# A new order of steps, W rows spread by TensorE, and no warm-up transposes in a three-network kernel

## The chip, the cores and the metric

The kernel runs on one core of one Trainium2 chip. The metric is the time of one execution on the device in microseconds (us). Five engines work side by side, each through its own queue in order: TensorE (PE: matmuls, with weight loads as PEld), VectorE (DVE), ScalarE (ACT), GpSimd (POOL) and SyncE (SP), which here issues all DMA transfers.

## The reference

Three parts follow one another. First a recurrent attention over 4 batches x 8 heads x 768 positions with head size 40:

```
m_new = max(f[t] + m, i[t])
C = exp(f[t] + m - m_new) * C + exp(i[t] - m_new) * outer(v[t], k[t])
n = exp(f[t] + m - m_new) * n + exp(i[t] - m_new) * k[t]
y[t] = sigmoid(o_gate[t]) * (C q[t]) / max(|n q[t]|, 1)
```

Its output, 3072 tokens x 320 features, goes into the first network: `h = x @ w_in` (320 to 1024), `s = h * softmax(h)`, a layer norm of s with gain `g_ln`, and `@ w_out` (1024 to 320). Then the second network: `g = x @ w_gate`, `val = x @ w_val` (320 to 1536 each), and `(silu(g) * val) @ w_out` (1536 to 320). Weights of the two networks come as 64-bit floats.

## The kernel before, in words

**Tiles.** The 768 positions are cut into 6 chunks of 128. A tile j is one chunk of one batch: j = 4 * chunk + batch, 24 tiles in all. Tiles 0 to 3 belong to the first chunk. In the second network four tiles (512 tokens) form a group g, and 128 of the 1536 hidden features form a slice f; a unit (g, f) is one of 6 x 12 = 72.

**The order is written by hand.** Every step is a small function, and the string ORDER (lines 28 to 101) lists which step is issued when, as `name:tile`, up to unit 18. A third number picks the engine for steps that can run on two: 0 is VectorE, 1 is GpSimd. After the string, `program` (line 104) goes on by rule: for each further unit gv, gt, gw, gy, yh, yl and then o2 of the unit before. Nothing reorders the steps later: each engine runs its share of this list in this sequence, and waits where an operand or a buffer isn't ready.

**The steps**, with the engine that runs them and the line in the profile:

- Gates of a chunk c: g0, g1, g2, gs (scans and small sums; L276 to L304), gd (store of the row gl to DRAM), gc and gx (transpose on PE, L318, then copy and exp into columns), er and ed (factors for the state).
- Decay weights W of a tile: gb loads the 8 rows gl of the tile from DRAM, spread over 128 partitions (512 KB, L340); gm masks them on GpSimd (L343); we takes 8 exponentials on ScalarE (L350).
- Attention of a tile: ld_qk, ld_vo, ld_qx, ld_e (loads); sc (scores on PE, L365), pm (times W on VectorE, L369), pv, pi, pd (matmuls, L377, L383, L391), cs, cd, ca (state), r0 to r2, ya, yb, yd (normalization, L420 to L439).
- First network of a tile: xT (transposes, L444), xh and xl (split in two parts of less precision), h (16 matmuls, L467), hx (maximum, DVE L471), he (exp, ACT), hu (DVE L480), z0, z1, zm, hc (DVE), hv (ACT), hr (GpSimd), uT (8 transposes, L513), uh and ul (split), o (24 matmuls, L530), oe, xd, x2, xc (output and transposes).
- Weights of the first network: w1l and w2l load them, five and four chunks; w1a to w1d and w2a to w2d turn the 64-bit pattern into float32 (ACT L183; DVE L187, L191, L196); w1h, w1o, w2h, w2o split them.
- Second network: vl, va to vd, vh, vo load, convert and split the weights of slice f (12 slices; vo is L678 and L680), Xh and Xl split the input, gv (16 matmuls, L707), gt, gw, gy (L711, L715, L719), yh, yl (L723, L727), o2 (12 matmuls, L737), ev (output). p2a and p2b mark where memory of the earlier parts becomes free for weights of the second network.
- wu: 8 transposes of the identity into a PSUM tile that nobody reads (L636). There are 18 of them.

**Buffers.** PSUM has two tiles of two banks, from `bank2` (they hold sc, h, uT and gv), and four of one bank, from `bank1`. A step that needs a slot waits for the last reader of the tile that held it. W has three slots in SBUF, qk and kvo four each.

The steps of the W path are these, and the change touches them:

```
def gb(j):
    c, b = divmod(j, B)
    T["W", j] = ak.tile([128, H, L], F32, tag="W", name="W", bufs=3)
    sp.dma_start(out=T["W", j], in_=gdr[c][b * H:(b + 1) * H, :].partition_broadcast(128))
```

Of the kernel before, what the change touches and what calls it, by code (L numbers as in the profile page):

```python
# [28 lines left out]
im w1l:0 ld_rows wu:0 ld_qk:0 w2l:0 wu:1 w1a:0 w1l:1 g0:0 w1b:0 g1:0:0 wu:2 g2:0 g0:1 gd:0 gs:0 w1c:0 ld_qk:1 wu:3  # L29
w2a:0 w1d:0 w2l:1 wu:4 w1h:0 w2b:0 w2c:0 w1o:0 gb:0 gc:0 sc:0 w1l:2 gx:0 w2d:0 w1a:1 g1:1 w1b:1 w2h:0 w1c:1 wu:5  # L30
ld_qk:2 w2a:1 g2:1 wu:6 w1d:1 w2b:1 w1h:1 wu:7 g0:2 gm:0 gb:1 w2c:1 w2l:2 wu:8 ld_vo:0 gs:1 we:0 w1o:1:0 gd:1 sc:1
w2d:1 w2o:0 wu:9 pm:0 w1a:2 gm:1 gb:2 wu:10 w2h:1 ld_qk:3 w1b:2 w1l:3 wu:11 g0:3 we:1 w1c:2 gc:1 w2o:1 w1d:2 pv:0
w2a:2 pm:1 er:1 gx:1 th:0 gm:2 gb:3 w1h:2 w2b:2 wu:12 ld_vo:1 w2c:2 g1:2 we:2 sc:2 r0:0 r1:0 r2:0 w2d:2 w1l:4 vw:0
ya:0 wu:13 yb:0 w1a:3 sc:3 pm:2 gm:3 gb:4 w2h:2 ld_qk:4 ib w1b:3 we:3 ld_vo:2 yd:0:0 w1c:3 pd:0 w2l:3 w2o:2 wu:14
w1o:2 w1d:3 xT:0 w1a:4 pv:1 vw:1 xh:0 w1b:4 w1h:3 cs:0 gm:4 th:1 w1c:4 ge:1 ld_qk:5 pd:1 r0:1 w1d:4 gb:5 w1o:3 sc:4
xl:0 w1h:4 ld_vo:3 g2:2 pm:3 vw:2 th:2 pv:2 gs:2 r1:1 w1o:4:0 w2a:3 we:4 r2:1 ld_qk:6 w2b:3 h:0 r0:2 ya:1 r1:2 cs:1
gm:5 yb:1 gb:6 gn:1 pm:4 yd:1 we:5 vw:3 ld_vo:4 r2:2 ed:1 ya:2 g1:3 xT:1 ld_qx:4 hx:0 gc:2 sc:5 gx:2 w2c:3 xh:1 pd:2
yb:2 ld_qk:7 w2d:3 pv:3 xl:1 gm:6 he:0 pd:3 ld_e:4 r0:3 we:6 r1:3 pv:4 hu:0 ld_vo:5 gb:7 pm:5 ld_qx:5 zm:0 sc:6 th:3
r2:3 z0:0 w2h:3 h:1 z1:0 pm:6 qw:4 ld_e:5 th:4 hc:0 gd:2 ld_qk:8 cs:2 hv:0 ya:3 yb:3 w2o:3 uT:0 ld_qx:6 pv:5 hx:1 uh:0
gb:8 vw:4 ld_vo:6 yd:2 ul:0 he:1 ld_e:6 gm:7 pi:4 th:5 qw:5:0 o:0 we:7 r0:4 g0:4 g2:3 hu:1 ld_qx:7 hr:0 zm:1:0 z0:1  # L40
ld_qk:9 cs:3 r1:4 gm:8 r2:4 sc:7 z1:1 ya:4 hc:1 pi:5 ld_vo:7 yb:4 gb:9 pd:4 we:8 r0:5 ld_qx:8 r1:5 uT:1 pm:7 ld_e:7
pv:6 r2:5 cd:4 er:2 qw:6 uh:1 ed:2 ya:5 ld_qk:10 sc:8 cs:4 vw:5 oe:0 yd:3:0 gd:3 hv:1 yb:5 pi:6 cd:5 ul:1 xT:2 vw:6
pd:5 gs:3:0 pv:7 xh:2 gm:9 gb:10 th:6 r0:6 ld_vo:8 xl:2 r1:6 ld_e:8 pm:8 h:2 we:9 r2:6 g1:4 ya:6 ld_qk:11 yb:6 th:7
ld_qx:9 qw:7:0 sc:9 ca:4 hx:2 xT:3 gm:10 o:1 pm:9 he:2 xd:0 ld_e:9 we:10 gb:11 cs:5 z0:2 hu:2 pi:7 hr:1 pv:8 ld_qk:12
z1:2 r0:7 ca:5 zm:2:0 r1:7 r2:7 ld_qx:10 hc:2 xh:3 vw:7 ld_vo:9 ya:7 th:8 sc:10 qw:8 er:3 xl:3 yb:7 uT:2 gm:11 g2:4
ld_e:10 pm:10 hv:2 gc:3 pi:8 gb:12 qw:9 pd:6 uh:2 h:3 hr:2 ul:2 gx:3 g0:5 r0:8 r1:8 r2:8 oe:1 ya:8 vw:8 ld_qk:13 we:11
cs:6 o:2 yb:8 cd:6 ld_e:11 hx:3 yd:4 gb:13 gm:12 ld_vo:10 gs:4:0 he:3 pd:7 x2:0 hu:3 pv:9 xc:0 g1:5 oe:2 ld_qk:14 z0:3
ca:6:0 we:12 ed:3 z1:3 cs:7 ld_qx:11 sc:11 zm:3 gd:4 cd:7 hc:3 pi:9 qw:10 xT:4 r0:9 sc:12 r1:9 xh:4 r2:9 ld_vo:11 vw:9
pm:11 pv:10 th:9 gb:14 ya:9 pd:8 pm:12 th:10 uT:3 yb:9 pi:10 ca:7 uh:3 xl:4 ge:2 h:4 r0:10 xd:1 th:11 qw:11 hv:3
yd:5:0 r1:10 vw:10 ld_qk:15 r2:10 gn:2 ya:10 cd:8 ld_e:12 ul:3 hr:3 ld_qx:12 gb:15 yb:10 o:3 gm:13 xd:2:0 hx:4 gm:14  # L50
cs:8 he:4 we:13 z0:4 hu:4 xT:5 sc:13 ld_qx:13 z1:4 g2:5 x2:1 ld_vo:12 zm:4 pv:11 hc:4 ld_e:13 oe:3 xh:5 we:14 xl:5
pd:9 pm:13 cd:9 ge:3 uT:4 gm:15 gb:16 pi:11 h:5 xd:3 ld_qx:14 r0:11 r1:11 cd:10 xc:1 r2:11 ld_vo:13 ya:11 uh:4
ld_qk:16 cd:11 yb:11 yd:6 ul:4 hv:4 ca:8:0 o:4 hx:5 th:12 we:15 hr:4 cs:9 ca:9 gm:16 qw:12:0 gn:3 x2:2 he:5 pd:10
# [757 lines left out]
```

## Time and profile before

| | |
|---|---|
| time, median of 3 runs | 765.88 us (765.79 to 766.67) |
| the profiled execution's own time | 765.78 us |
| its span, first to last instruction | 764.1 us |
| mean granted TensorE clock | 0.982 |
| TensorE busy | 738.7 us, 97% |
| VectorE busy | 444.2 us, 58% |
| ScalarE busy | 327.1 us, 43% |
| GpSimd busy | 176.1 us, 23% |

The profile is of one execution. Busy time is the union of an engine's instructions; matmuls overlap one another at their ends, so the spacing of their starts is their cost in a dense stretch, and it is less than the duration of one. The granted clock is given as a share of 2.4 GHz; its two levels are 1.00 and 0.50.

### The profile page before, as it was taken

How to read it: one execution, taken by the hardware profiler on the slowest of the kernel's cores; microseconds unless marked ns; L12 is line 12 of the kernel's file. 1: busy time of each engine (PE TensorE's matmuls, PEld its weight loads, DVE VectorE, ACT ScalarE, POOL GpSimd, SP SyncE). 2: the span in 40 equal slices, each digit the busy share in tenths (PEclk: the TensorE clock that was granted, in tenths of full speed). 3: DMA queues.
4: the chain of work that ended last, by engine and by line, in shares of the span. 5: the costliest groups of instructions: out<-in, count | busy, mean ns of one | idle time of the engine just before them, and what ended most of it. 6: DMA issues, size and time to landing. Idle time of an engine off the chain costs nothing. (4 is left out here: it accounts for less than half of the span.)

```text
span 764.1 us, 11503 instructions
## 1 busy us (share of the span) xinstructions
PE 738.7 (97%) x4478; PEld 658.1 (86%) x4478; DVE 444.2 (58%) x753; ACT 327.1 (43%) x675; POOL 176.1 (23%) x237
## 2 busy tenths in 40 slices
...
GB/s 235 313 231 176 236 229 146 136 277 95 139 110 68 77 104 104 103 54 51 9 148 1 0 35 1 1 35 0 1 35 1 0 1 36 1 0 36 1 1 34
DMA packets 24279, 62.31 MB, mean 82 GB/s; under 512 B 3195, under 2 KB 11488, under 8 KB 24224
## 3 DMA queue, kind: packets, MB, share of 16 engines
...
q8 instruction: 35, 0.57, 0.3%
...
## 5 line engine op out<-in xcount | busy, mean ns | idle before, releaser
L707 PE MATMUL a<-Xh,w 128*128 128x512 f32 x720 | 237.8, 395 | 3.5 <-DVE t L719 2.6
L707 PE MATMUL a<-Xl,w 128*128 128x512 f32 x432 | 169.8, 393 | 0.0
L707 PEld LDWEIGHTS a<-Xh,w 128*128 128x128 f32 x720 | 132.2, 188 | 29.5 <-ACT w L674 2.3
L715 DVE SCALAR_TENSOR_TENSOR t<-t,a 128x512 f32<-128x512 f32 x72 | 49.5, 687 | 167.4 <-ACT t L711 167.4
L737 PE MATMUL c<-w,yh 128*128 128x320 f32 x576 | 127.9, 309 | 1.1 <-ACT yh L723 1.1
L711 ACT ACTIVATE t<-a 128x512 f32<-128x512 f32 x72 | 43.0, 598 | 166.1 <-PE a L707 164.9
L737 PEld LDWEIGHTS c<-w,yh 128*128 128x128 f32 x576 | 99.1, 188 | 7.3 <-ACT yh L723 1.4
L707 PEld LDWEIGHTS a<-Xl,w 128*128 128x128 f32 x432 | 81.3, 188 | 19.3
L737 PE MATMUL c<-w,yl 128*128 128x320 f32 x288 | 89.0, 309 | 0.2 <-DVE yl L727 0.2
L723 ACT ACTIVATE yh<-t 128x512 fp32r<-128x512 f32 x72 | 45.5, 632 | 100.7 <-DVE t L719 100.7
L727 DVE TENSOR_TENSOR yl<-t,yh 128x512 fp32r<-128x512 f32 x60 | 43.2, 720 | 38.5 <-ACT yh L723 38.5
L530 PE MATMUL c<-wo_h,uh 128*128 128x320 f32 x192 | 60.5, 315 | 0.1
L350 ACT ACTIVATE W<-W,col 128x128 f32<-128x128 f32 x192 | 58.4, 393 | 4.9 <-POOL W L343 4.9
L530 PE MATMUL c<-wo_h,ul 128*128 128x320 f32 x192 | 59.6, 311 | 0.7 <-DVE ul L521 0.7
L467 PE MATMUL a<-wi_h,xh 128*128 128x512 f32 x144 | 59.6, 414 | 0.2 <-DVE P L369 0.2
L530 PE MATMUL c<-wo_l,uh 128*128 128x320 f32 x192 | 59.3, 309 | 0.0
L467 PE MATMUL a<-wi_h,xl 128*128 128x512 f32 x144 | 57.8, 401 | 0.0
L737 PEld LDWEIGHTS c<-w,yl 128*128 128x128 f32 x288 | 54.1, 188 | 0.4 <-DVE yl L727 0.4
L719 DVE SCALAR_TENSOR_TENSOR t<-t,a 128x512 f32<-128x512 f32 x72 | 49.4, 687 | 2.4
L377 PE MATMUL c<-kvo,P 128*128 128x41 f32 x384 | 49.1, 291 | 1.7 <-issue 1.7
L377 PEld LDWEIGHTS c<-kvo,P 128*128 128x128 f32 x384 | 48.1, 204 | 2.3 <-issue 1.8
L369 DVE TENSOR_TENSOR P<-a,W 128x1024 f32<-128x1024 f32 x24 | 29.1, 1214 | 24.3 <-PE a L365 16.3
...
## 6 DMA issues: line engine op xcount, KB each, us to landing
...
```

The lines of the kernel that those rows point to most:

```text
L350: act.activation(g[:, h, :], g[:, h, :], AF.Exp, bias=cols[c][:, b * H + h:b * H + h + 1])
L369: dve.tensor_tensor(out=T["P", j], in0=T["S", j].rearrange("p (h n) -> p h n", h=H), in1=T["W", j], op=ALU.mult)
L377: pe.matmul(po[:, h * D1:(h + 1) * D1], P[:, h, :], vn[:, h, :], start=h == 0, stop=j < B and h == H - 1)
L467: pe.matmul(ph[:, fs], x, w[:, fs], start=n == 0, stop=n == 7)
L530: pe.matmul(po[:, 0:DM], x[:, fs], w[:, f, :], start=n == 0, stop=n == 3 * KF - 1)
L707: pe.matmul(p[:, s * 512:s * 512 + GT], w, x, start=n == 0, stop=n == 7)
L711: act.activation(T["t", g, f], T["gv", g, f][:, 0:GT], AF.Tanh, scale=0.5)
L715: dve.scalar_tensor_tensor(out=t, in0=t, scalar=1.0, in1=p[:, 0:GT], op0=ALU.add, op1=ALU.mult)
L719: dve.scalar_tensor_tensor(out=t, in0=t, scalar=0.5, in1=p[:, 512:512 + GT], op0=ALU.mult, op1=ALU.mult)
L723: act.activation(T["yh", g, f], T["t", g, f], AF.Copy)
L727: alu[e].tensor_tensor(out=T["yl", g, f], in0=T["t", g, f], in1=T["yh", g, f].bitcast(F32), op=ALU.subtract)
L737: pe.matmul(T["acc", g][t][:, 0:DM], x[:, ts], w, start=f == 0 and n == 0, stop=f == KF2 - 1 and n == 2)
```

## The change

The ORDER string is replaced up to unit 18. The set of steps is the same but for the 18 wu, which go, together with their function. Many small steps change their engine number: in sum VectorE takes from GpSimd four g1, one gs, one w1o, three vo, four yl, six zm and two yd, and gives it five ca, four xd and two qw. `gd:0`, the store of the first chunk's gl, stays, although no load reads it any more.

For the tiles 0 to 3, W is made differently. gb no longer loads: it runs 8 matmuls into a two-bank PSUM tile, each with one column of the identity, repeated 128 times, as the stationary operand and gl of the chunk as the moving one, so that each row of gl appears on all 128 partitions. we reads that PSUM tile and writes W in SBUF, and gm masks after the exponential, with 0 as fill instead of -1e30. In the code:

```diff
     def gb(j):
         c, b = divmod(j, B)
+        if j < NP:
+
+            T["gw", j] = bank2()
+            for h in range(H):
+                n = b * H + h
+                pe.matmul(T["gw", j][:, h * L:(h + 1) * L], ident[0:BH, n:n + 1].to_broadcast([BH, 128]), T["gl", c],
+                          start=True, stop=True)
+            return
         T["W", j] = ak.tile([128, H, L], F32, tag="W", name="W", bufs=3)
         sp.dma_start(out=T["W", j], in_=gdr[c][b * H:(b + 1) * H, :].partition_broadcast(128))
 
     def gm(j):
+
         pool.affine_select(out=T["W", j], in_=T["W", j], pattern=[[0, H], [1, L]], compare_op=ALU.is_ge,
-                           fill=NEG, base=0, channel_multiplier=-1)
+                           fill=0.0 if j < NP else NEG, base=0, channel_multiplier=-1)
 
     def we(j):
         c, b = divmod(j, B)
+        if j < NP:
+            T["W", j] = ak.tile([128, H, L], F32, tag="W", name="W", bufs=3)
         g = T["W", j]
+        x = T["gw", j].rearrange("p (h n) -> p h n", h=H) if j < NP else g
         for h in range(H):
-            act.activation(g[:, h, :], g[:, h, :], AF.Exp, bias=cols[c][:, b * H + h:b * H + h + 1])
+            act.activation(g[:, h, :], x[:, h, :], AF.Exp, bias=cols[c][:, b * H + h:b * H + h + 1])
...
-    def wu(n):
-        p = bank1()
-        for i in range(8):
-            pe.transpose(p[:, (i % 4) * 128:(i % 4 + 1) * 128], ident, ident)
```

(`NP` is 4, `BH` is 32 rows.) The new order begins like this, up to the first h:

```
w1l:1 w1l:0 g0:0 g1:0:0 w2l:0 ld_rows w1a:1 w1a:0 g2:0 w1b:1 w1c:1 w1d:1 gb:1 w1b:0 w2a:0 ib gs:0 ld_qk:1 w1c:0 w1h:1
w1l:2 gc:0 w2l:2 ld_vo:0 w2b:0 gx:0 g0:1 w2c:0 g0:2 g1:1:0 w2d:0 g2:1 gs:1:0 gb:0 we:1 we:0 w1o:1 w2h:0 gm:1 sc:1 gm:0
pm:1 w1d:0 gc:1 w2a:2 gb:2 ld_qk:0 ld_vo:1 we:2 w2b:2 w2c:2 w2o:0 w1a:2 w1h:0 w2d:2 gb:3 vw:0 gx:1 w2h:2 pd:0 w2l:1
w1b:2 gd:1 sc:0 w1o:0:0 pm:0 ld_vo:2 ld_qk:2 pv:1 ld_qk:3 w1l:4 pv:0 im w2a:1 w2o:2 cs:0 w1c:2 w2b:1 w1d:2 w2c:1 r0:0
we:3 vw:1 w1l:3 gm:2 r1:0 pd:1 er:1 ld_vo:3 w2d:1 sc:2 vw:2 r0:1 gb:4 th:0 r2:0 ld_qk:4 sc:3 r1:1 ya:0 gm:3 ed:1 r2:1
ld_vo:4 pm:2 g1:2 w2h:1 ge:1 cs:1 yb:0 w1a:4 w2o:1 pm:3 yd:0:0 vw:3 w1b:4 pd:2 gn:1 pv:2 w1c:4 cs:2 w1a:3 th:2 xT:0
r0:2 th:1 ya:1 gd:0 w1d:4 gb:5 yb:1 ld_qx:4 pv:3 xh:0 w1b:3 pd:3 r1:2 w1h:2 xl:0 w1h:4 gm:4 r2:2 ya:2 yd:1 ld_e:4
w1c:3 we:4 w1d:3 w1o:2:0 xT:1 w1h:3 yb:2 w1o:4 ld_qk:5 th:3 g2:2 ld_vo:5 sc:4 w1o:3:0 g0:3 gb:6 h:0 pm:4 gs:2 xh:1
```

From there on the first network's tiles and the attention of later tiles are interleaved as before. From `x2:2 he:5 pd:10` on (line 53 before) the two orders run the same steps, up to `h:11 zm:10:0 z1:10` (line 69 before), except for wu and for the engine of some ca; then they differ again.

## Rows read from the trace of the kernel before

**Rows 1.** The page's busy line: us (share of the span) and instructions of each engine.

```profile
PE 738.7 (97%) x4478; PEld 658.1 (86%) x4478; DVE 444.2 (58%) x753; ACT 327.1 (43%) x675; POOL 176.1 (23%) x237
```

**Rows 2.** Chain of waits, in order of time: start us, us, what.

```profile
461.57 3.74 PE a L707 x16
```

**Rows 3.** Windows: stretch, busy us (instructions) of each engine, clock, DMA share, GB/s.

```profile
0.00:100.00 100.00, 86.25 (x635) 79.28 (x636) 75.81 (x154) 56.86 (x150) 57.46 (x75) 0.86 0.75 237
0.00:10.00 10.00, 7.41 (x40) 7.18 (x40) 4.31 (x15) 1.96 (x2) 3.27 (x11) 1.00 0.66 202
20.00:30.00 10.00, 2.35 (x14) 2.12 (x12) 7.34 (x14) 4.97 (x15) 9.68 (x6) 0.72 1.02 345
30.00:40.00 10.00, 10.00 (x59) 8.89 (x60) 8.28 (x13) 9.81 (x31) 9.43 (x15) 0.50 0.84 289
60.00:70.00 10.00, 10.00 (x44) 8.61 (x44) 5.44 (x11) 1.15 (x2) 4.94 (x8) 0.57 0.71 200
372.00:420.00 48.00, 45.23 (x228) 38.71 (x229) 43.91 (x52) 26.98 (x48) 19.96 (x15) 1.00 0.17 62
```

**Rows 4.** Timeline of TensorE, first 42 us: start us, us, instruction, [idle before].

```profile
1.42 7.41 PE L636 MATMUL c<-ident 128*128 128x128 f32 x40 [1.42 <-POOL ident masks.py:199]
...
12.68 3.71 PE L636 MATMUL c<-ident 128*128 128x128 f32 x32
...
27.90 0.42 PE L318 MATMUL c<-ident,st 96*128 96x96 f32 x1 [7.65 <-POOL st L304]
28.12 3.53 PE L377 MATMUL c<-kvo,P 128*128 128x41 f32 x16
...
33.32 2.08 PE L365 MATMUL a<-qk 40*128 40x128 f32 x16
...
39.24 1.51 PE L391 MATMUL c<-vw,kvo 128*120 128x123 f32 x6
```

**Rows 5.** Timeline of TensorE, 139 to 142 us: the step sc:14.

```profile
141.24 0.94 PE L365 MATMUL a<-qk 40*128 40x128 f32 x12
```

**Rows 6.** Timeline of TensorE, 64 to 83 us: first rows of steps from h:1 on.

```profile
64.60 0.79 PE L467 MATMUL a<-wi_h,xh 128*128 128x512 f32 x1
...
70.28 1.03 PE L513 MATMUL a<-ident,e 128*128 128x128 f32 x8
...
73.53 0.39 PE L530 MATMUL c<-wo_h,uh 128*128 128x320 f32 x1
...
77.22 1.16 PE L365 MATMUL a<-qk 40*128 40x128 f32 x16
78.31 0.90 PE L383 MATMUL c<-C,qT 120*128 120x123 f32 x6
79.05 0.80 PE L391 MATMUL c<-vw,kvo 128*120 128x123 f32 x6
79.68 1.04 PE L513 MATMUL a<-ident,e 128*128 128x128 f32 x8
80.56 1.88 PE L377 MATMUL c<-kvo,P 128*128 128x41 f32 x16
82.36 1.16 PE L365 MATMUL a<-qk 40*128 40x128 f32 x16
```

**Rows 7.** Waits over the span: us in total, times, longest us.

```profile
POOL W L343 <- DMA W<-gd: 15.8, 7, 7.4
```

**Rows 8.** Timeline of SyncE: the last load of the first network's w_in.

```profile
25.64 0.33 SPq L564 DMA_DIRECT2D x2T<-in_w_in_dram  x1
```

**Rows 9.** Timeline of ScalarE: the exponentials of tile 0.

```profile
20.01 2.45 ACT L350 ACTIVATE W<-W,col 128x128 f32<-128x128 f32 x8 [0.73 <-POOL W L343]
```

**Rows 10.** Instruction groups of VectorE, first 100 us: count | busy us, mean ns | idle before.

```profile
L369 DVE TENSOR_TENSOR P<-a,W 128x1024 f32<-128x1024 f32 x10 | 12.1, 1214 | 7.7 <-POOL lf L285 4.2 <-PE a L365 3.5
...
L471 DVE TENSOR_REDUCE nm<-a 128x1 f32<-128x1024 f32 x3 | 3.7, 1222 | 2.8 <-PE a L467 2.8
```

**Rows 11.** Timeline of TensorE at 402 us, with its wait.

```profile
402.18 0.70 PE L707 MATMUL a<-Xh,w 128*128 128x512 f32 x2 [0.96 <-DVE t L719]
```

More of the change, by code (lines that the diff above doesn't have):

```diff
@@ L28 @@
 ORDER = """
[L29 to L53, printed above, removed]
@@ new lines @@
+th:5 r2:5 pi:6 gb:9 ca:5 oe:0 th:7 ld_qx:8 vw:6 uh:1 xh:3 ld_qk:10 qw:7 gm:8 ld_qk:9 r0:6 pv:7 ya:5 gm:10 vw:7 yb:5
+gc:3 he:2 th:6 ul:1 pi:7 sc:8 we:8 r0:7 xl:3 cd:7 r1:6 ld_e:8 ld_qx:11 er:3 o:1 hu:2 z0:2 pm:8 we:10 ld_vo:10 gm:9
+r2:6 gb:11 ld_e:10 z1:2 cd:6 ya:6 xd:0:0 yb:6 pd:6 zm:2:0 gx:3 th:8 x2:0 hr:1 sc:10 r1:7 qw:8 ld_e:9 yd:4:0 r2:7 sc:9
+hc:2 cs:6 ld_qx:10 we:9 ld_qk:12 g1:4:0 pv:8 ld_qk:11 pm:10 oe:1 uT:2 pi:8 ya:7 ca:6 pm:9 g0:5 r0:8 xT:4 xc:0 uh:2 h:3
+r1:8 ul:2 ge:2 gm:11 yb:7 hv:2 qw:10 yd:5:0 gn:2 xd:1:0 hx:3 th:10 he:3 pv:10 ld_qx:9 hu:3 r2:8 pd:7 pi:10 zm:3 xh:4
@@ new lines @@
+qw:12 ul:4 ya:9 ld_vo:12 yd:6:0 ld_vo:13 ld_qk:15 ya:11 h:5 yb:11 ld_qx:14 th:12 xd:3 ld_e:13 cd:9 ca:9:1 o:4 we:14
+hx:5 gm:16 yb:9 x2:2 he:5 pd:10 vw:11 ld_qk:17 sc:14 oe:4 qw:13 hu:5 xc:2 pd:11 vw:12 pv:12 z0:5 z1:5 cs:10 er:4
+zm:5:0 ca:10 hc:5 ed:4 ld_e:14 xT:6 pm:14 gd:5 pi:12 xh:6 th:13 pv:13 ld_qx:15 hv:5 cs:11 r0:12 qw:14 ld_e:15 sc:15
+r1:12 xl:6 ca:11 r2:12 uT:5 pm:15 vw:13 pi:13 ya:12 x2:3 ld_qx:16 yd:7:0 h:6 r0:13 yb:12 yd:8 xc:3 ld_e:16 hr:5 uh:5
+yd:9:0 r1:13 ld_vo:14 yd:10 gb:17 cd:12 ul:5 ld_qk:18 qw:15 pd:12 hx:6 o:5 th:14 vw:14 ld_vo:15 r2:13 cs:12 ya:13
@@ new lines @@
+yb:13 gb:18 xT:7 oe:5 he:6 gc:4 pv:14 xh:7 z0:6 gx:4 xl:7 we:16 gm:17 hu:6 ld_vo:16 pd:13 ld_qk:19 ca:12 sc:16 z1:6
+cd:13 pi:14 th:15 pm:16 zm:6 xT:8 cd:14 sc:17 r0:14 gs:5 r1:14 pv:15 ld_vo:17 r2:14 ya:14 ld_e:17 we:17 yb:14 gb:19
+ld_qx:17 h:7 gm:18 hc:6 qw:16 hv:6 pm:17 th:16 yd:11:0 cs:13 ca:13 uT:6 hx:7 xh:8 pd:14 gm:19 yd:12:0 xl:8 he:7 pi:15
+hr:6 xT:9 pv:16 uh:6 vw:15 hu:7 vw:16 yd:13:0 xd:4:0 r0:15 ul:6 h:8 we:18 z0:7 r1:15 r2:15 zm:7:0 cs:14 yd:14:0 z1:7
+ya:15 ld_qk:20 yb:15 we:19 gb:20 pi:16 ld_e:18 x2:4 ld_vo:18 r0:16 hc:7 o:6 ld_qx:18 xc:4 hx:8 th:17 xh:9 hv:7 r1:16
@@ new lines @@
+xl:9 r2:16 ya:16 ld_qk:21 hr:7 yb:16 uT:7 oe:6 xd:5 gc:5 ge:4 uh:7 pd:15 pv:17 vw:17 gn:4 gx:5 ul:7 er:5 he:8 cd:15
+ed:5 qw:17 ca:14 o:7 ld_qx:19 z0:8 hu:8 gm:20 cs:15 zm:8:0 z1:8 sc:18 x2:5 pm:18 pi:17 xT:10 sc:19 r0:17 r1:17 gb:21
+hc:8 ld_qx:20 h:9 xc:5 pm:19 ld_vo:19 ld_e:19 r2:17 ya:17 yb:17 xd:6:0 hv:8 gb:22 uT:8 hx:9 xh:10 qw:18 ld_qk:22 oe:7
+pv:18 uh:8 xd:7:0 gm:21 ld_e:20 he:9 ul:8 x2:6 pi:18 we:20 o:8 yd:15:0 hu:9 xc:6 z0:9 xl:10 zm:9 hr:8 z1:9 sc:20 oe:8
+xd:8 xT:11 pm:20 h:10 th:18 hc:9 gb:23 th:19 ld_qx:21 qw:19:0 hv:9 r0:18 r1:18 ld_e:21 r2:18 ya:18 yb:18 uT:9 xh:11
@@ new lines @@
+hx:10 uh:9 xl:11 pd:16 he:10 ul:9 cd:16 x2:7 ld_vo:20 pd:17 gm:22 ld_qk:23 we:21 o:9 ca:15 cs:16 vw:18 z0:10 hu:10
+vw:19 cd:17 yd:16:0 ca:16 gm:23 cs:17 h:11 zm:10:0 z1:10 xT:12 hr:9 hc:10 we:22 uT:10 oe:9 ca:17:1 hv:10 xh:12 uh:10
+th:20 xd:9:0 hx:11 xc:7 xl:12 ul:10 xT:13 pv:19 he:11 pd:18 x2:9 hu:11 sc:21 pi:19 qw:20:0 ld_e:22 z0:11 hr:10 pm:21
+z1:11 zm:11 r0:19 cs:18 h:12 o:10 cd:18 xh:13 qw:21 hc:11 hx:12 r1:19 ld_qx:23 hv:11 uT:11 xc:9 uh:11 r2:19 xl:13
+ul:11 pv:20 oe:10 pi:20 ca:18 he:12 z0:12 hr:11 ld_qx:22 x2:8 hu:12 o:11 r0:20 zm:12:0 z1:12 ld_vo:21 oe:11 hc:12
@@ new lines @@
+hv:12 ya:19 uT:12 h:13 uh:12 pd:19 r1:20 ld_vo:23 yb:19 xc:8 cd:19 yd:18 ul:12 hx:13 r2:20 pd:21 xT:14 cs:19 he:13
+o:12 xd:11 hu:13 pd:20 ya:20 xh:14 xl:14 xd:10:0 z0:13 yb:20 x2:11 pv:21 zm:13 pi:21 z1:13 hr:12 hc:13 uT:13 th:21
+ld_e:23 uh:13 th:23 r0:21 xc:11 ul:13 hv:13 h:14 we:23 r1:21 hx:14 oe:12 he:14 z0:14 hu:14 ld_vo:22 qw:23 xT:15 o:13
+sc:22 xh:15 z1:14 xl:15 hr:13 sc:23 pm:22 r2:21 yd:19 ca:19:1 x2:10 pm:23 zm:14:0 oe:13 hc:14 xT:16 h:15 ya:21 hx:15
+yb:21 xc:10 xh:16 uT:14 hv:14 pv:22 he:15 hu:15 xl:16 uh:14 pv:23 z0:15 pi:23 zm:15:0 ul:14 z1:15 r0:23 hc:15 pd:22
```

82 lines of the change are left out of this document (34 added, 48 removed).

## Prediction

> **What bounds the kernel now.** I read the page's busy line first: TensorE is busy for 738.7 of 764.1 us [rows 1], so the end can only come earlier by what TensorE wastes. The chain of waits says where it cannot: from the unit that follows the hand-written order, at 461.57 us, matmuls follow one another to the end, 16 of them in 3.74 us [rows 2]. That stretch is the same code after the change, so the whole effect is a shift of the moment at which it begins.
>
> Before that moment TensorE has about 400 us of work at its dense pace, so some 58 us go elsewhere. The windows show where. Until 70 us the engine is starved or slow: in 20:30 it works 2.35 of 10 us, and the granted clock is 0.50 in 30:40 and 0.57 in 60:70, the lower of its two levels, 1.2 GHz, for all or most of these stretches [rows 3]. The timeline shows that the early "busy" is largely the warm-up transposes, 40 of them in the first row, and that the first real matmuls of the head wait 7.65 us for a GpSimd result [rows 4].
>
> The step sc:14 (scores of tile 14) is a useful mark. It starts at 141.24 us [rows 5]; from just before it both orders run the same 295 steps, up to tile 12 of the first network, but for the warm-ups and the engine of a few small updates. Ahead of it stand 14 sc, 12 pv, 11 pd, 8 pi, 6 h, 5 uT, 5 o and a few small steps: by the spacing of full-clock rows (sc 1.09, pi 0.74, pd 0.63, uT 0.88, pv 1.80, o 3.69 [rows 6], h 3.74 as the same 16 matmuls of [rows 2]) about 98 us. So 43 of the 58 us are lost before the mark, and the rest after it.
>
> **What the change does, part by part.**
>
> *W rows by TensorE.* Four loads of 512 KB leave a queue whose DMA engines are 0.66 to 1.02 busy in the head [rows 3]; GpSimd's mask waited 15.8 us in all for such loads, up to 7.4 us for one [rows 7]. In SyncE's order these loads also stood ahead of weight loads: one weight load is only issued at 25.64 us [rows 8]. In the new order all five w1l, and everything else up to the mask of tile 3, is issued without a wait for W. The fifth weight load then has 6.8 MB with it and ahead of it: 2.0 MB move in the first 10 us (202 GB/s), the rest at the 345 GB/s of 20:30 takes 14 us [rows 3], so it lands near 24 us, ahead of its use at some 31. In their place come 4 x 8 matmuls, which the trace doesn't have. The nearest row is sc, also eight matmuls with 128 output columns: 1.09 us at full clock [rows 6], 2.0 at half (33.32, 2.08 with its overlap [rows 4]). Below: nothing, if they fill idle time. I take 2.0 each, since they come in the cold head, and they lie on TensorE's way to h:0. The exponentials move ahead of the mask and read PSUM; eight took 2.45 us from SBUF [rows 9], I keep that (bounds: half of it, or a quarter more; ScalarE isn't the last to arrive either way). A late store of the gates (gd:0) that nobody reads stays, at nothing: SyncE has idle time there.
>
> *The warm-ups.* Fifteen of 18 stand in the head, where TensorE waits for others anyway: in time alone they are worth nothing. Three stand at 159, 212 and 292 us in dense work, 0.88 us each (eight transposes, as uT [rows 6]): **2.6 us** gained.
> What else they did is the clock. The first 40 transposes took 7.41 us, 0.185 each, where 32 later ones took 3.71, 0.116 each [rows 4]: the engine began slow, though the granted clock reads 1.00 from the start [rows 3], and had become faster before the real work. Without them the head begins slow and, as I take it, stays so until h:0. The Trainium skill (TensorE: Matmul & The Clock Gate, section "Why this matters for your kernels") warns of just this: gaps between bursts of matmuls put the clock back to half, and it advises warming up first. The trace agrees in that the idle stretch before 27.90 us is followed by 0.50 in 30:40. By that rule alone the change would lose; its price is the last rival's.
>
> *The new order in the head.* It pulls the attention of tiles 0 to 3 and all weight chunks ahead, and moves small steps (g1, gs, most w1o) from GpSimd to VectorE. VectorE becomes what bounds the head. h:3 needs the PSUM slot that pm:9 frees, and by then VectorE has 169 instructions behind it. In before's first 100 us it ran 154 in 75.81 us of busy time [rows 3], 0.492 each (large ones, as pm, 1.21, hx 1.22 [rows 10], with many small): 169 x 0.492 = **83.2 us**. After pm:9 TensorE has, up to the mark, 3 h, 3 o, 3 pv, 3 sc, 4 pd, 3 pi, 2 uT and 1.3 us of small steps: 11.2 + 11.1 + 5.4 + 3.3 + 2.5 + 2.2 + 1.8 + 1.3 = **38.8 us** [rows 2, 6]. The same sum from h:4, behind pm:12, comes out alike; later steps have slack.
>
> The open term is VectorE's idle time up to pm:9. Below: 5.7 us, the idle part of its first 10 us (4.31 busy [rows 3]), since rows and first weights come as before. Above: 24.2, all its idle time in before's first 100 us. I followed the queues: 5.5 us at the start; then VectorE has converted weights and multiplied tiles to fall back on until h:0. TensorE's cold work ahead of h:0 is 4 gb and 5 sc at 2.0, 4 pv at 3.3 (28.12 to the next row), 4 pd at 1.5 and 1.6 of small steps: 38.8 us [rows 4], nearly all behind the first two exponentials (about 16 us), so h:0 starts near 49 and, begun slow, takes 5.7 (h:1, 64.60 to 70.28 [rows 6]). VectorE would be ready some 6.5 us before it ends. Another 1.5 us are round trips hx, he, hu, with nothing queued between. Sum **13.5 us**.
>
> The mark then falls at 83.2 + 13.5 + 38.8 = 135.5 us, **5.7 us** earlier.
>
> *After the common stretch* the order is new from tile 12 to unit 18. VectorE takes over some 10 us more than it did in all. The tight place is 372:420, where it is busy 43.91 of 48 us with 52 instructions and TensorE 45.23 [rows 3], and TensorE waits for its result (0.96 us at 402.18 [rows 11]). From the opening of the last weight pool to unit 10, VectorE's queue has 44 instructions now and 55 then, for 38 and 42 us of TensorE's work: at 0.844 each, 37 and 46 us. Some of the 55 may come late without harm. Bounds: 4 us lost (46 against 42), or 3 gained (the idle 2.8 of that window closed). I take **1.0 us lost**. Elsewhere the pairs of transposes and copies have about the slack that they have now.
>
> **The sum.** It is made against the profiled execution's own 765.78 us (span 764.1 and 1.7 around it), 0.1 below the median: 765.8 - 5.7 - 2.6 + 1.0 = **758.5 us**.
>
> **Rivals.**
>
> 1. *The head is not slowed by TensorE.* If the cold matmuls keep ahead of VectorE, its idle time nears 5.7: 7.8 us less, 750.7. For it: h runs 3.74 when warm, and transfers are lighter. Against: from 28 to about 40 us, attention matmuls and transposes ran back to back at half pace (3.53, 2.08 and 1.51 us [rows 4], against 1.80, 1.09 and 0.63 [rows 6]).
> 2. *The starvation stays.* VectorE idles as now, for another reason (fewer transfers, but waits for cold matmuls at each tile): at 21 us idle the gain is gone, 766; at 24.2 us it is 769. For it: 24.2 is what the head does today; against: what was waited for, W and late weights, goes.
> 3. *Slower: the clock.* Half clock from h:0 through h:2. TensorE has 22 us of full-clock work there, 45 at half, against VectorE's 26 and its waits of about 2: 17 us more, 775. It turns the sign once the slow clock costs VectorE 7.3 us more than in the sum. For it: the clock is 0.57 in 60:70 [rows 3], where the steps are like those between h:0 and h:2. Against: h:1, begun there, took 5.7 us and not twice 3.74, so the clock came back within it.
> 4. *The last weights bound.* 4 us lost there in place of 1: 761.5, still faster.
>
> **Chances.** The sum's way, with idle time of 8 to 18 us and rival 4 within it, 753 to 763: 0.56. Rival 1: 0.19. Rival 2: 0.15, of which 0.05 still faster, 0.09 within 0.2% (1.5 us, about what this measurement can tell) and 0.01 beyond. Rival 3: 0.10. Faster 0.80, same 0.09, slower 0.11. The range leaves out 2 in 10 and reaches from 750.5 (the lower bound of idle time) to 766 (idle time at which the gain is gone).
>
> **What would show it.** Right: sc:14 starts between 132 and 139 us; VectorE busy over 85% of 10:45; the granted clock 0.50 from the first matmuls to about 50 us; weight loads all issued by 15 us; three gaps of 0.88 us closed; TensorE's idle time in 350:420 as now. Wrong: sc:14 after 141 (rivals 2, 3; the clock tells which), before 130 (rival 1), or a difference after 220 us that is larger than the one at the mark.

## The result, and the profile after

| | before | after |
|---|---|---|
| time, median | 766.27 us (765.79 to 767.83, 4 runs) | 774.66 us (772.01 to 776.06, 4 runs) |
| the profiled execution's own time, its span | 765.78, 764.1 us | 776.06, 774.1 us |
| sc:14, the mark, starts | 141.24 us | 146.65 us |
| first unit behind the written order starts | 461.41 us | 471.35 us |

The ratio is 1.0102 (95% interval 1.0071 to 1.0133): the change made the kernel slower by 1%. The forecast, 758.5 us with a range to 766, was wrong by 16 us and on the wrong side.

The page's busy line after, and the row of the chain of waits that answers to [rows 2]:

```profile
PE 744.7 (96%) x4398; PEld 661.1 (85%) x4398; DVE 454.9 (59%) x779; ACT 324.3 (42%) x675; POOL 149.0 (19%) x211
```

```profile
471.51 3.74 PE a L713 x16
```

TensorE has 80 matmuls fewer than in [rows 1] (144 transposes less, 64 records of gb more, two for each of its 32 matmuls) and is busy 6 us longer, so its work ran more slowly. The chain is the same pure TensorE to the end, 9.94 us later. So the shift of the end is again the whole effect. Windows after (us of PE, PEld, DVE, ACT, POOL with instructions, clock, DMA share, GB/s):

```profile
0.00:100.00 100.00, 87.92 (x526) 80.79 (x526) 77.85 (x157) 51.48 (x139) 44.17 (x60) 0.97 0.64 202
...
20.00:30.00 10.00, 10.00 (x53) 9.63 (x53) 6.09 (x9) 6.20 (x21) 2.57 (x3) 1.00 0.81 281
30.00:40.00 10.00, 10.00 (x54) 9.63 (x54) 7.49 (x16) 2.89 (x9) 4.61 (x6) 1.00 0.40 106
60.00:70.00 10.00, 10.00 (x76) 8.56 (x76) 7.82 (x19) 8.60 (x27) 4.54 (x7) 1.00 0.65 203
80.00:90.00 10.00, 7.66 (x39) 6.67 (x38) 8.58 (x20) 1.89 (x5) 2.81 (x3) 0.66 0.34 93
350.00:420.00 70.00, 64.89 (x344) 55.71 (x342) 56.75 (x73) 37.37 (x64) 18.20 (x20) 1.00 0.21 71
```

TensorE is now without a gap in 20:30, where it had idled [rows 3], yet VectorE is less busy there, and in 30:40, than before. The timeline of TensorE tells why; the first rows of steps:

```profile
5.16 3.75 PE L343 MATMUL a<-gl,ident 32*128 32x128 f32 x16 [5.16 <-DVE gl L289]
...
19.63 0.42 PE L317 MATMUL c<-ident,st 96*128 96x96 f32 x1 [3.47 <-DVE st L303]
19.98 7.19 PE L343 MATMUL a<-gl,ident 32*128 32x128 f32 x32
27.11 1.51 PE L402 MATMUL c<-vw,kvo 128*120 128x123 f32 x6
28.55 2.08 PE L376 MATMUL a<-qk 40*128 40x128 f32 x16
30.56 7.05 PE L388 MATMUL c<-kvo,P 128*128 128x41 f32 x32
...
58.34 0.63 PE L478 MATMUL a<-wi_h,xh 128*128 128x512 f32 x1
58.77 0.56 PE L478 MATMUL a<-wi_h,xl 128*128 128x512 f32 x1
59.17 0.39 PE L478 MATMUL a<-wi_h,xh 128*128 128x512 f32 x1
```

```profile
82.86 0.79 PE L455 MATMUL c<-ident,y 128*128 128x128 f32 x3 [2.34 <-DVE y L446]
83.58 2.08 PE L376 MATMUL a<-qk 40*128 40x128 f32 x16
```

(Full pace and half pace are the two clock levels as the spacing of the rows shows them: twice the time for the same row is half pace.) From 19.98 us to the start of h:0 at 55.62, TensorE works without a break and at half pace: pv takes 3.4 us, sc 2.0, and the two gb 3.55 each, against 1.8 for pv and 1.09 for sc at full pace [rows 6]. In the middle of h:0, at 59 us, the spacing falls to that of full pace. (The clock column reads 1.00 all the while; the durations say otherwise.) At 80.5 us TensorE waits 2.34 us for VectorE, and behind that wait it works at half pace again, to 89.8 us, with 0.66 in 80:90.

Up to the end of pm:9, the step that my sum used, this is VectorE's window and the largest of its waits (us in total, times, longest):

```profile
0.00:106.90 106.90, 94.46 (x597) 86.92 (x598) 83.91 (x173) 55.84 (x153) 46.27 (x62) 0.97 0.64 203
```

```profile
DVE wc L186 <- ACT wc L182: 5.2, 3, 1.9
DVE P L380 <- PE a L376: 3.9, 2, 2.7
DVE rc L431 <- PE c L388: 2.9, 2, 1.7
DVE nm L482 <- PE a L478: 2.1, 1, 2.1
DVE rc L431 <- PE c L394: 2.0, 2, 1.7
```

It was busy 83.9 us, and idle 23.0. VectorE's own timeline says where it waits for TensorE up to the end of h:0:

```profile
30.75 1.22 DVE L380 TENSOR_TENSOR P<-a,W 128x1024 f32<-128x1024 f32 x1 [2.73 <-PE a L376]
37.65 0.17 DVE L431 TENSOR_SCALAR rc<-c 128x8 f32<-128x8 f32 x1 [1.72 <-PE c L388]
47.84 0.17 DVE L431 TENSOR_SCALAR rc<-c 128x8 f32<-128x8 f32 x1 [1.15 <-PE c L388]
61.24 1.22 DVE L482 TENSOR_REDUCE nm<-a 128x1 f32<-128x1024 f32 x1 [2.09 <-PE a L478]
```

Three waits for attention matmuls (sc is L376, pv L388) make 5.6 us, and the wait for h:0 itself 2.1. The rest is 5.9 us of waits up to 11 us, 2.7 for ScalarE and GpSimd ahead of h:0, 1.2 in the round trips hx, he, hu, 4.2 from 85 us on, and 1.4 in small gaps.

In the kernel before, pm:9 ends at 93.3 us, with 70.8 busy and 22.5 idle: the new order put 13.1 us of VectorE's work more ahead of pm:9, and took nothing off its waits. In return the way from the end of pm:9 to the mark is shorter: 39.8 us against 47.9.

From the mark to the end of the written order, the steps of TensorE show two differences from before. The stretch up to uT:23, near 365 us, is 0.7 us shorter (221.3 us against 222.0), although the three late warm-ups, 2.6 us, are gone from it; the run before_bare below shows why. From there to unit 18 another 5.2 us are lost. With the 5.4 at the mark that is 5.4 - 0.7 + 5.2 = 9.9, the shift that the chain shows.

### The profile page after: what moved, and what is told of

Its sections match the earlier page's. It is cut to its first block, busy times and chain, and to the rows that moved or that the text cites. A ratio compares the mean times of both kernels' runs of the same rounds, so it can differ in the third digit from the quotient of the medians.

```text
span 774.1 us, 11307 instructions
## 1 busy us (share of the span) xinstructions
PE 744.7 (96%) x4398; PEld 661.1 (85%) x4398; DVE 454.9 (59%) x779; ACT 324.3 (42%) x675; POOL 149.0 (19%) x211
## 4 chain that ended last, share of the span: by engine, by line
PE 82%; DVE 11%; ACT 3%; issue 2%; DMA 1%; SPq 0%; POOL 0%; ACTq 0%; DVEq 0%
PE a L713 31%; PE c L743 14%; PE a L478 11%; PE c L541 9%; PE c L388 6%; PE a L376 3%; PE a L524 2%; PE c L402 2%; DVE cc L190 1%; PE c L455 1%; PE c L394 1%; DVE t L721 1%; DMA x2T<-in_w_out_dram 1%; DVE nm L482 1%; PE a L343 1%
## 5 line engine op out<-in xcount | busy, mean ns | idle before, releaser
L388 PE MATMUL c<-kvo,P 128*128 128x41 f32 x384 | 52.4, 303 | 0.3 <-DVE xl L467 0.3
L388 PEld LDWEIGHTS c<-kvo,P 128*128 128x128 f32 x384 | 51.3, 215 | 1.6 <-DVE xl L467 0.8
L361 ACT ACTIVATE W<-W,col 128x128 f32<-128x128 f32 x160 | 48.6, 392 | 4.5 <-POOL W L351 4.4
L482 DVE TENSOR_REDUCE nm<-a 128x1 f32<-128x1024 f32 x24 | 29.3, 1223 | 24.2 <-PE a L478 24.1
```

The lines of the kernel that those rows point to most:

```text
L361: act.activation(g[:, h, :], x[:, h, :], AF.Exp, bias=cols[c][:, b * H + h:b * H + h + 1])
L388: pe.matmul(po[:, h * D1:(h + 1) * D1], P[:, h, :], vn[:, h, :], start=h == 0, stop=j < B and h == H - 1)
L482: dve.tensor_reduce(out=T["nm", j], in_=T["h", j], axis=AX.X, op=ALU.max, negate=True)
```

## The experiments

All kernels compute the whole result. Each ratio is against the kernel before, run on the same chip (its medians there: 766.2 to 767.0 us). The last column is from one profiled execution. Four of these kernels have the same order up to sc:14 (changed kernel, new_head_old_tail, after_old_end, after_tail_engines), and theirs stands at 146.65, 146.23, 144.77 and 143.41: a difference of 3 us in this column is not clear.

| kernel | median us | ratio (95% interval) | sc:14 |
|---|---|---|---|
| changed kernel | 774.66 | 1.0102 (1.0071 to 1.0133) | 146.65 |
| before_bare | 763.18 | 0.9942 (0.9921 to 0.9964) | 139.11 |
| before_bare_spread | 768.35 | 1.0019 (1.0003 to 1.0036) | 144.75 |
| bare_gates_dve | 762.86 | 0.9937 (0.9913 to 0.9960) | 139.73 |
| new_head_old_tail | 769.94 | 1.0043 (1.0019 to 1.0068) | 146.23 |
| after_old_end | 771.42 | 1.0089 (1.0060 to 1.0117) | 144.77 |
| after_warm | 772.19 | 1.0060 (1.0037 to 1.0083) | 142.22 |
| after_loads | 775.07 | 1.0088 (1.0058 to 1.0118) | 147.31 |
| after_head_engines | 778.81 | 1.0146 (1.0108 to 1.0184) | 153.14 |
| after_tail_engines | 781.54 | 1.0177 (1.0145 to 1.0210) | 143.41 |
| after_yb4 | 773.92 | 1.0089 (1.0057 to 1.0121) | 143.22 |
| after_hot | 767.74 | 1.0018 (0.9987 to 1.0049) | 139.79 |
| bare_hot | 762.00 | 0.9964 (0.9934 to 0.9994) | 137.68 |
| bare_hot2 | 763.82 | 0.9970 (0.9949 to 0.9991) | 143.72 |
| hot_loads_old_tail | 764.52 | 0.9982 (0.9952 to 1.0013) | 141.24 |
| hot_head_old_tail | 760.31 | 0.9917 (0.9885 to 0.9949) | 139.62 |
| hot_head_old_tail_yb4 | 758.56 | 0.9909 (0.9873 to 0.9945) | 135.27 |

**before_bare.** All wu taken out of the order before:

```diff
-im w1l:0 ld_rows wu:0 ld_qk:0 w2l:0 wu:1 w1a:0 w1l:1 ...
+im w1l:0 ld_rows ld_qk:0 w2l:0 w1a:0 w1l:1 ...
```

> The kernel before without its 18 warm-up steps, all else as it was. Theory 1 (they carry the clock of the head): sc:14 comes 4 to 10 us later than 141.24, and in spite of three gaps of 0.88 us closed the time is 767 to 773. Theory 2 (my prediction's step: in time alone the 15 early ones are worth nothing): sc:14 at 140 to 142 and the time 2.6 us below the kernel before, near 763.3.

The time fell by 0.6%, to what theory 2 gave, but not by its sum. TensorE does the head at half pace and reaches h:0 2.5 us later, at 50.28, yet sc:14 comes 2.1 us earlier; the stretch at 0.57 in 60:70 [rows 3] is absent from this profile. The three late warm-ups are worth 0.9 us and not 2.6: from the mark to the last matmul the profiles have 618.4 us without them and 619.3 with them. Where one stood at 292 us, TensorE now waits 1.72 us instead of 0.85, and at 211 us it waits 0.57 us where it had not waited: two of the three had mostly filled waits. In the old order the transposes gained no time.

**after_warm.** 64 transposes put into the idle places of the new head:

```diff
-... w1d:1 gb:1 ... sc:1 ... gc:1 ...
+... w1d:1 wu wu wu gb:1 ... wu sc:1 ... wu wu wu wu gc:1 ...
```

> The changed kernel with eight warm-up steps of eight transposes put back where TensorE idles in its head: three ahead of the first gb, one ahead of sc:1, four ahead of gc:1 (64 transposes). Nothing else differs. Theory 1 (the clock): the head is late because TensorE, without transposes, works at half pace until 59 us; then the spacing of the gb rows falls from 3.6 to about 1.8 us, h:0 begins near 46 us instead of 55.6, and sc:14 comes 6 to 11 us earlier than its 146.65, at 136 to 141; time 764 to 769. Theory 2 (the order itself, VectorE's queue): sc:14 stays at 144 to 148 and the time at 772 to 776, whatever the clock does.

Between the theories: sc:14 4.4 us earlier, the time 2.5 us less (the intervals of the two ratios overlap). TensorE's timeline shows where the effect ends:

```profile
27.75 1.98 PE L390 MATMUL c<-kvo,P 128*128 128x41 f32 x16
30.13 2.96 PE L390 MATMUL c<-kvo,P 128*128 128x41 f32 x16 [0.40 <-DVE P L382]
32.89 1.49 PE L404 MATMUL c<-vw,kvo 128*120 128x123 f32 x6
34.31 3.79 PE L378 MATMUL a<-qk 40*128 40x128 f32 x32
```

The pv at 27.75 still runs at full pace, the next one loses it halfway, and the rest of the head runs at half pace (0.50 in 40:50), though TensorE had worked almost without a gap since 16 us.

**after_loads.** The matmuls of gb undone:

```diff
-    NQ, NP = 4, 4
+    NQ, NP = 4, 0
-... g2:0 w1b:1 ... we:1 we:0 ... gm:1 sc:1 gm:0 ...
+... g2:0 gd:0 w1b:1 ... gm:1 gm:0 ... we:1 sc:1 we:0 ...
```

> The changed kernel with W of tiles 0 to 3 loaded from DRAM as in the kernel before (gd:0 right behind g2:0, the mask again ahead of the exponentials); order and missing warm-ups as in the changed kernel. Theory 1 (the matmuls of gb are dear: four times 3.6 us of slow TensorE, of which gb:2 and gb:3, 7.1 us, stand in a dense stretch): sc:14 comes about 7 us earlier, near 140, and the time is near 767. Theory 2 (loads bring back the wait that the matmuls removed; 15.8 us of mask waits in the kernel before): sc:14 stays at 145 to 150 or comes later, time 773 to 779.

Theory 2: in this order the loads cost what the slow matmuls cost. TensorE is busy 2.28 and VectorE 2.10 of the 10 us in 20:30; GpSimd waits 8.1 us for one W, and TensorE 9.5 us for a result of GpSimd that comes behind it.

**before_bare_spread.** The matmuls of gb alone, in the old order without warm-ups (we ahead of gm for tiles 0 to 3).

> The kernel before without warm-ups (763.2 us, sc:14 at 139.1), and with W of tiles 0 to 3 spread by TensorE; order and engines as before. Theory 1 (the spread trades a wait for loads for slow matmuls, and either costs the same, as in the changed kernel): sc:14 at 138 to 141, time 762 to 765. Theory 2 (what my prediction had: the loads are what starves the head): TensorE's idle 10.5 us ahead of 27.7 are filled, sc:14 comes 3 to 6 us earlier, 757 to 760.

Both theories fell: it lost 5.2 us. TensorE's timeline of this kernel:

```profile
21.39 3.78 PE L344 MATMUL a<-gl,ident 32*128 32x128 f32 x16 [6.93 <-ACT W L362]
25.77 2.08 PE L377 MATMUL a<-qk 40*128 40x128 f32 x16 [0.61 <-DVE P L381]
27.79 3.77 PE L344 MATMUL a<-gl,ident 32*128 32x128 f32 x16
31.49 0.42 PE L318 MATMUL c<-ident,st 96*128 96x96 f32 x1
31.70 3.53 PE L389 MATMUL c<-kvo,P 128*128 128x41 f32 x16
35.16 3.78 PE L344 MATMUL a<-gl,ident 32*128 32x128 f32 x16
```

The first row is gb:1. It needs the slot of two banks that gb:0 holds until ScalarE's exponentials have read it, and waits 6.93 us; gb:2 and gb:3 stand in the dense stretch at 3.7 us each, and h:0 moves from 50.28 to 55.76.

**bare_gates_dve.** `g1:1 gs:1` become `g1:1:0 gs:1:0` in before_bare.

> The kernel before without warm-ups, with g1 and gs of chunk 1 on VectorE instead of GpSimd (seven small steps), as the new order has them. Theory 1 (GpSimd's queue is what the head waits for: VectorE idles 4.2 us for a result of it in the first 100 us, TensorE 10.5 us): sc:14 comes 2 to 5 us earlier than 139.1, time 758 to 761. Theory 2 (those seven steps, some 3 us of VectorE, only move the wait): sc:14 at 138 to 141, time 762 to 765.

Theory 2. The transposed columns come 5 us earlier on TensorE, which then waits for pm:0.

**after_head_engines** and **after_tail_engines.** The new order with the old engine numbers, on the 26 steps up to z1:10 that differ, and on the 38 behind it:

```diff
-... g1:1:0 ... gs:1:0 ... w1o:0:0 ... yd:2:0 ... zm:0:0 ...
+... g1:1 ... gs:1 ... w1o:0 ... yd:2 ... zm:0 ...
```

> The changed kernel with the engine numbers of the kernel before on the 26 steps up to z1:10 whose number differs (g1, gs, most w1o, yd, zm and others back on GpSimd; some ca, qw back on VectorE); the order stays. Theory 1 (VectorE's load sets the head: up to the end of pm:9 it is busy 83.9 us in the changed kernel and 70.8 in the kernel before, with the same idle time of some 23): 5 to 7 us of the 13 leave VectorE, pm:9 ends near 101 instead of 106.9, sc:14 comes near 141, time 769 to 771. Theory 2 (what is moved to GpSimd comes back as a wait for it): VectorE is less busy and idles as much more, sc:14 stays within 2 us of 146.6, time 773 to 777.

> The changed kernel with the engine numbers of the kernel before on the 38 steps behind z1:10 whose number differs (yl, vo, zm, yd, xd among them). Theory 1 (the tail's 4.7 us come from the steps that VectorE takes over): 2 to 4 us of them come back, 770.5 to 772.5. Theory 2 (they come from the sequence in which the steps are queued): nothing comes back, 774 to 777.

Theory 1 fell in both, and both came out slower than theory 2 allowed: 4 and 7 us lost (for the first, the intervals of the two ratios just overlap). In the head 6.9 us did leave VectorE's work ahead of pm:9 (77.0), and 5.5 came back as idle time (28.5), among it 4.3 for GpSimd's masks; pm:9 ends 1.4 us earlier, and sc:14 comes 6.5 us later all the same. Near 125 us VectorE waits 4.37 us for GpSimd's part of g1, which stands behind a mask that waited 5.19 us for a load of W, and TensorE then waits 6.43 us for VectorE. In after_tail_engines the stretch from the mark to uT:23 is 6.4 us longer, and the one from uT:23 on, at 402.5 us, is that of the changed kernel. So the moves to VectorE are not what made the change slow: with the old engine numbers the new order is slower still.

**new_head_old_tail** and **after_old_end.** The order before from z1:10 on, and from p2b on.

> The changed kernel up to z1:10 (the end of the common stretch), then the order of the kernel before, without its last warm-up. Theory 1 (the new tail loses by itself, 4 to 5 us by the steps of TensorE between 363 us and unit 18): 769 to 771, with sc:14 unchanged near 146.6. Theory 2 (the tail only loses because the head left VectorE late): the old tail loses as much, 773 to 776.

> The changed kernel up to p2b, where the last pool of weights opens, and the 157 steps behind it up to unit 18 in the sequence and with the engine numbers of the kernel before. Theory 1 (the tail's 4.7 us are lost behind p2b, where TensorE waits for gy, yl and the output copy): 770 to 772. Theory 2 (they are lost ahead of it, and the waits behind only follow): 774 to 777.

The new tail loses 4.7 us by itself. From uT:23 to the last matmul the profiles have 402.5 us in the changed kernel and 402.5 to 402.6 in the six others with its sequence there, after_tail_engines among them; with the old tail it is 397.3 (before, before_bare, new_head_old_tail). So these 5.2 us come with the sequence and not with the engine numbers. after_old_end has 401.0: only 1.6 of the 5.2 lie behind p2b, although its median is 3.2 us lower and in theory 1's range; its ratio can't be told from the changed kernel's. TensorE's longest waits of the changed kernel there (first rows behind a wait), and VectorE's largest wait in 363:471:

```profile
393.15 0.42 PE L743 MATMUL c<-w,yl 128*128 128x320 f32 x1 [0.88 <-DVE yl L733]
403.80 0.41 PE L743 MATMUL c<-w,yl 128*128 128x320 f32 x1 [1.37 <-POOL yl L733]
410.77 0.70 PE L713 MATMUL a<-Xh,w 128*128 128x512 f32 x2 [1.50 <-DVE t L725]
...
450.44 0.56 PE L743 MATMUL c<-w,yh 128*128 128x320 f32 x2 [1.59 <-ACT ob L749]
```

```profile
DVE t L721 <- ACT t L717: 31.6, 8, 6.6
```

VectorE isn't short of time there: it waits 31.6 us for ScalarE's silu (29.0 in the kernel before, in 363:461). From uT:23 to unit 18 TensorE idles 6.7 us, against 3.0 before. It waits for single results: of the chain gv, gt, gw, gy, yh, yl, and once for the output copy ev. These waits are 3.7 of the 5.2 us; that the new sequence asks for the results too soon after they were begun is my reading of the order, and no run moves them one by one.

**after_hot.** Wide matmuls into PSUM tiles that the next step overwrites:

```diff
+    def hot(p, n):
+        for i in range(n):
+            pe.matmul(p[:, 0:512], wz[:, 0:128], wz, start=True, stop=True)
     def sc(j):
         ps, t = bank2(), T["qk", j]
+        hot(ps, {1: 2, 0: 4, 2: 4, 3: 4, 4: 4}.get(j, 0))
...
```

(`wz` is a tile of ones in bfloat16; gc, gb and pv get such a line too.)

> The changed kernel with wide matmuls added that nobody reads (a 128x128 by 128x512 product of ones in bfloat16, written into a PSUM tile that the next step overwrites): eight ahead of gc:1, two or four each ahead of gb:2, gb:3, sc:0 to sc:4 and pv:0 to pv:3, 46 in all, some 10 us of TensorE at full pace. Theory 1 (TensorE's half pace is what holds the head, and wide matmuls keep the clock up where transposes did not): gb takes 1.8 us, pv 1.7 to 1.8 and sc 1.1 from 20 us on, h:0 begins near 46 to 50 us instead of 55.6, sc:14 comes 4 to 9 us earlier than 146.65, time 766 to 771. Theory 2 (the clock falls all the same, or VectorE sets the head and the added matmuls are time lost): h:0 begins at 55 to 62, sc:14 at 146 to 155, time 774 to 783.

Theory 1. Rows of TensorE:

```profile
20.11 2.05 PE L352 MATMUL a<-gl,ident 32*128 32x128 f32 x16
...
28.22 1.88 PE L399 MATMUL c<-kvo,P 128*128 128x41 f32 x16
...
34.13 1.16 PE L386 MATMUL a<-qk 40*128 40x128 f32 x16
...
50.13 0.50 PE L489 MATMUL a<-wi_h,xh 128*128 128x512 f32 x1
```

gb takes 2.0 us, pv 1.7, sc 1.1, although 46 matmuls were added; h:0 begins 5.5 us earlier, sc:14 6.9, and the time falls by 6.9. VectorE's idle time up to pm:9 goes from 23.0 to 15.7 us, its work stays (84.5). This is the run that shows the cause: the edit only gives TensorE more work, which nobody needs, its pace rises, and the time falls.

**bare_hot** and **bare_hot2.** The same in bare_gates_dve, with 34 and with 48 of them.

> The kernel before without warm-ups and with g1 and gs of chunk 1 on VectorE (762.9 us, sc:14 at 139.7), and with 34 such wide matmuls: ten ahead of gc:1 and eight ahead of pv:0, where TensorE is idle, and three or four ahead of pv:1, pv:2 and sc:2 to sc:4. Theory 1: full pace from 27 us on, h:0 near 44 to 47 instead of 50.5, sc:14 2 to 5 us earlier, time 758 to 761, the fastest so far. Theory 2 (VectorE sets the head there): h:0 is earlier and sc:14 is not; time 762 to 765.

> The kernel before without warm-ups and with g1 and gs of chunk 1 on VectorE, with wide matmuls as in the run at 762.0 us, but twenty instead of eight ahead of pv:0 and four instead of three ahead of sc:2 and sc:3, so that TensorE has no idle gap before 28 us. Theory 1 (there the clock fell after the 2.6 us gap ahead of pv:0): attention matmuls at full pace from 28 us on, h:0 near 46, sc:14 at 135 to 137, time 758.5 to 761. Theory 2 (VectorE sets that head, busy 75 of the 90 us up to pm:9): h:0 earlier, sc:14 at 137 to 139, 761 to 763.

Both miss: the time doesn't tell them from bare_gates_dve. The pace didn't hold in either: in the first it is lost during the pv at 26.61, behind a wait of 2.64 us for kvo; in the second, behind one of 1.74 us at 27.68, though 19 wide matmuls had just run. (The profile of bare_hot2 is of its slowest execution, 767.36 us; its sc:14 says little.) What a lasting full pace is worth in the old order stays open.

**hot_head_old_tail** and **hot_loads_old_tail.** after_hot with the old tail, and the same with `NP = 0` as in after_loads.

> The changed kernel with the wide matmuls in its head (767.7 us) and, behind z1:10, the order of the kernel before without its last warm-up. Theory 1 (the pace of the head and the sequence of the tail are two separate losses): the two gains of 6.9 and 4.7 us add up, 762 to 764, equal to the kernel before without warm-ups (763.2), so that the new order of the head then neither gains nor loses. Theory 2 (they overlap): 765 to 768.

> As the last one, but W of tiles 0 to 3 loaded from DRAM (gd:0 right behind g2:0, mask ahead of the exponentials), with the wide matmuls of gb left out. Theory 1 (the matmuls of gb lose by their place on a slow TensorE; at 2.0 us each they are cheaper than the wait for the loads): with loads the head idles 7 to 10 us ahead of 28 us, as it did in the changed kernel with loads, and the time is 2 to 5 us above that of the last one. Theory 2 (the spread loses in itself, as it lost 5.2 us in the order before): 2 to 5 us below it, 758 to 761.

The two losses are separate: 774.66 - 6.9 - 4.7 = 763.1 was due, and 760.31 came, 1.7 us under theory 1's range. It is below before_bare's 763.18, but the intervals of the two ratios overlap. And W by TensorE gains 4.2 us at full pace by the medians; the two profiled executions differ by only 1.3. With loads, TensorE's wait is back:

```profile
26.93 1.51 PE L413 MATMUL c<-vw,kvo 128*120 128x123 f32 x6 [5.80 <-POOL vw L376]
```

**after_yb4** and **hot_head_old_tail_yb4.** One step moved, because xT:3 waits for the slot that yb:4 frees:

```diff
-ya:4 w2h:3 w2o:3 ul:0 yb:4
+ya:4 yb:4 w2h:3 w2o:3 ul:0
```

> The changed kernel with one small step moved: yb:4, which frees the PSUM slot that xT:3 waits for, stands ahead of w2h:3 and w2o:3 (2.60 us on VectorE) and ul:0 instead of behind them. Theory 1 (TensorE's idle 2.34 us at 80.5 us come from that queue position, and the clock's second fall behind them, too): the gap closes to under 0.5 us, the granted clock stays at 1.00 in 80:90, sc:14 comes 3 to 6 us earlier, time 769 to 772. Theory 2 (the next step waits instead, o:0 for ul:0 behind the same 2.60 us; the clock falls all the same): sc:14 within 1.5 us of 146.65, time 773 to 776.

> The fastest so far (wide matmuls in the new head, old tail; 760.3 us) with yb:4 moved in the same way. Theory 1: 2 to 4 us less, 756.5 to 758.5. Theory 2: 759.5 to 762.

In both profiles the clock stays at 1.00 in 80:90 and sc:14 comes 3.4 and 4.4 us earlier, but the gap isn't closed: 1.65 us before sc:7 and 0.38 before o:0 take its place. The times hardly follow: 774.66 to 773.92, and 760.31 to 758.56, the lowest median here; neither ratio can be told from that of the kernel it started from. In after_yb4's profile 2.4 of the 3.4 us are lost again behind the mark, in a stretch where the clock falls without any gap:

```profile
270.00:285.00 15.00, 15.00 (x95) 14.67 (x94) 8.00 (x20) 5.86 (x10) 1.83 (x6) 0.77 0.36 133
```

The changed kernel has 1.00 at these steps. In the faster one the gain is kept there. That the gap at 80 us makes the clock fall isn't shown: after_tail_engines has the same wait (2.33 us) and kept 1.00 in 80:90, with TensorE busy 7.89 of 10 us.

## Why the prediction was wrong

**The head's idle time: the step that failed.** The sum was 83.2 us of VectorE's work up to pm:9, 13.5 idle, 38.8 behind it. Measured: 83.9, 23.0 and 39.8. The work and the remainder were right within 1 us; the idle time was 9.5 us too small. I had counted 8.0 us of waits behind the start: 6.5 for h:0 (2.1 in fact) and 1.5 of round trips (1.2 in fact), and nothing at the matmuls ahead of h:0, nor behind h:2. There VectorE waits tile by tile: 5.6 us for sc and pv ahead of h:0, and 4.2 from 85 us on, behind the second slow stretch. after_hot gives the cause its size: at full pace 7.3 us of this idle time are gone. This is my second rival, "the starvation stays", in its own words "for another reason (fewer transfers, but waits for cold matmuls at each tile)"; it had 15 in 100. By its own price 23.0 us of idle time give 768 us. The rest, to the profiled 776, is mainly the tail (4.2 us more than forecast), the late warm-ups (1.7 less gained) and 1.7 in VectorE's work and the way to the mark.

**The price of gb.** I took sc as the nearest row, 2.0 us at half pace. It was 3.55, so four of them cost 14.3 us and not 8. The nearer row stood in the same group: pv, 16 records in 3.33 us [rows 4], 0.21 each, as gb's 0.22. sc's eight matmuls alternate between two partition ranges (0 and 64) and cost 0.13; gb and pv do not alternate. That this is the reason was not tested. h:0 began at 55.62 and not near 49; the 6.3 us of gb are nearly the whole difference.

**The warm-ups.** "In time alone worth nothing" was too kind to them: without all 18 the old order is 3.8 us faster by the medians, 3.0 by the profiles, 2.1 of it at the mark. The term of 2.6 us for the late three was mis-sized; they gave 0.9. The Trainium skill's rule (TensorE: Matmul & The Clock Gate, section "Why this matters for your kernels": keep TensorE busy, warm up, avoid gaps) weighed against the change, and the change lost. The runs agree with it in that the pace of this head was worth 6.9 us. They differ in that the old order gained without its warm-ups, and in that 35.6 us without a gap didn't bring the full pace. In after_warm transposes brought it, and the work that followed didn't hold it.

**The slower rival** (the third in the list; the prediction's "last rival" means this one). Half clock from h:0 through h:2 did not occur; the pace returned within h:0, fell once more behind h:2, and returned within o:0. The 775 us were right for another reason.

**W rows by TensorE.** I had the loads as what starves the head. Undoing only that changes nothing (775.07). W by TensorE is worth 4.2 us at full pace (1.3 by the profiles), and costs 5.2 in the old order at half pace. Its sign went with the pace; in the old order the slot that gb:0 holds cost 6.93 us of waiting besides, and no run separates the two.

**The tail.** I took 1.0 us lost, with a bound of 4, from VectorE's count of instructions. It lost 5.2 in the profile and 4.7 in the runs, beyond the bound, 3.7 of it in TensorE's waits for single results; the count was the wrong measure, as VectorE idles there.

**The signs.** sc:14 came after 141. VectorE was busy 26.2 of 35 us in 10:45, 75% and not over 85. TensorE's idle time in 350:420 grew from 3.9 to 5.1 us. The last two weight loads were issued at 22.12 us and not by 15, still ahead of their use. Half pace did last from the first matmuls, to 59 us. The three late gaps closed, for 0.9 us. And the loss behind the common stretch is there, as the sign for "wrong" had it: the difference from before grows from 5.4 us at the mark to 9.9.
